# Sigmoid attention and a gated feed-forward on one core: attention moved ahead of the feed-forward and computed in unsplit float32 on four 64x64 array tiles

## The chip, the cores and the metric

The kernel runs on one core of a Trainium2 chip (trn2). The metric is device time in microseconds (us), the median of three runs. The kernel before takes 1445.89 us (1444.95 to 1446.85).

Engines are named as in the profile: PE is TensorE (matrix products), PEld its weight loads, DVE is VectorE, ACT is ScalarE, POOL is GpSimd, SP is SyncE, whose queue issues every DMA of both kernels. SBUF is the on-chip memory with 128 partitions; PSUM holds the results of PE, in 8 banks of 512 float32 columns per partition. `F32R` is a float32 format that PE takes in one pass and that keeps fewer bits than float32. The kernels keep float32 accuracy by splitting a value into a high and a low F32R part and adding three products (low x high, high x low, high x high).

## What is computed

There are 8 batches, 12 heads, 448 positions, head size 64, so 3584 tokens of 768 features; the hidden size is 1536.

```python
def _attn_ref(q, k, v) -> np.ndarray:
    S = q.shape[2]
    scale = 1.0 / np.sqrt(q.shape[-1])
    scores = scale * np.matmul(q, k.transpose(0, 1, 3, 2)) - np.log(S)
    attn = 1.0 / (1.0 + np.exp(-scores))
    return np.matmul(attn, v).astype(np.float32)

def _moe_ref(x, w_gate, w_val, w_out) -> np.ndarray:
    gate = 1.0 / (1.0 + np.exp(-(x @ w_gate)))
    val = x @ w_val
    return (gate * val @ w_out).astype(np.float32)
```

The attention output, heads side by side, is `x` of the feed-forward. There is no softmax: the attention weight of a key is a sigmoid, so keys can be taken in any groups and their products summed. The three weight matrices arrive as float64, viewed as 64-bit integers; the kernel turns them into F32R pairs by bit operations ("conversion").

## The kernel before, in words

**Hidden tiles.** The hidden size is cut into 12 tiles of 128. For a block of tokens, `ff_in` makes one hidden tile: for gate and value each 18 products (6 feature tiles x 3 terms), then a sigmoid on ACT, a product on DVE, and the split of the result into `hh` and `hl`. `ff_out` makes one of 6 output tiles from 3 products per hidden tile. The weights of 12 tiles don't fit in SBUF beside the attention, so the feed-forward is done in two passes over the tokens: the first `J1 = 5` tiles with their partial output written to DRAM (`part`), then the other 7 tiles, where `add` loads the partial output and sums.

**First stage (L272 to L461).** `heads` runs the attention head by head. The first 12 heads (`N32 = 12`, one batch) use float32 as it is: q and k stand twice in the 128 partitions, which gives twice the score, so the scale is halved. The other 84 heads are split: `split` makes F32R parts on DVE and POOL, `scores` issues 2 products for each of 4 key blocks of 128, ACT applies the sigmoid twice (once to F32R, once in place in PSUM), DVE subtracts to get the low part, and `values` issues 7 products. That makes 15 products of 448 columns for each head. `merge` mixes these heads with the first feed-forward pass, in blocks of 448 tokens, one batch behind. The head counts of each part are fixed by `HEADS_IN` and `HEADS_OUT`.

**Conversion.** `convert` handles half a row block of one matrix (128x384 elements): seven DVE operations on the words, and an eighth, `finish_lo`, that makes the low part (L137). With `spread`, the last step goes to ACT and POOL (L134, L135) and the high part is copied by ACT (L150). Each conversion loads the words of a later one (`load_words`, L98, two buffers). In the first 12 heads one conversion follows each step, so that the 5 tiles are converted early; 5 more tiles are then converted and written to DRAM (`convert_ahead`).

**Second stage (L464 to L547).** The last 448-token block of the first pass is finished, the remaining two tiles are converted, and the 5 stored tiles are fetched. Then 7 blocks of 512 tokens run through 7 hidden tiles: per block 7 x 36 + 6 x 21 = 378 products of 512 columns. `load_x` reads the attention output from DRAM and `split_x` makes its two F32R parts.

**What sets the order.** Each engine executes its queue in order. A planner orders the instructions of each queue by what they depend on; an instruction given to `keep_in_program_order` keeps its place in the written order. Buffers of a pool are handed on when their last reader has finished.

Of the kernel before, what the change touches and what calls it, by code (L numbers as in the profile page):

```python
# [11 lines left out]
U32 = mybir.dt.uint32  # L12
# [6 lines left out]
P = 128  # L19

F64_ZERO = 2.0 ** -15

J1 = 5

N32 = 12

NA = 5

EV, EW = 14, 2
# [3 lines left out]
HEADS_IN, HEADS_OUT = (23, 36, 48), (24, 38, 50)  # L33
# [3 lines left out]
def sigmoid_attention_glu_kernel(ctx: ExitStack, tc: tile.TileContext, qk, v, wg, wv, wo, out):  # L37
# [7 lines left out]

    nc = tc.nc
    B, H = qk.shape[0], qk.shape[1]
# [3 lines left out]
    NT = T // TB  # L51
    NP = H // 2
    SK = qk.shape[3] - S
# [4 lines left out]
    HP = P // 2  # L58
    scale = 1.0 / math.sqrt(D)
    J2 = NJ - J1  # L60

    const = ctx.enter_context(tc.tile_pool(name="const", bufs=1))
    wpool = ctx.enter_context(tc.tile_pool(name="wpool", bufs=1))
    work = ctx.enter_context(tc.tile_pool(name="work", bufs=2))
    dram = ctx.enter_context(tc.tile_pool(name="dram", bufs=1, space=DRAM))
    mm = ctx.enter_context(tc.tile_pool(name="mm", bufs=2, space=PSUM))
# [3 lines left out]
    x_dram = [dram.tile([P, T], F32, name=f"xd{c}") for c in range(NP)]  # L70
    w_dram = {j: [dram.tile([P, 2, DM], F32, name=f"wd{j}_{t}") for t in range(3)] for j in range(J1, J1 + NA)}
    part = [dram.tile([P, T], F32, name=f"part{o}") for o in range(NO)]


    wgv, wos = {}, {}
    KC = KT // 2

    def chunks(j, t):
        w = (wg, wv, wo)[t]
        return [w[j][:, c * KC * P:(c + 1) * KC * P] for c in range(2)]  # L80

    late = list(range(J1, NJ))
    n_own = J2 - J1


    order = [(i, o, 0) for i in range(n_own) for o in (False, True)]
    order += [(i, False, i - n_own + 1) for i in range(n_own, J2)]
    order += [(i, True, J1 + 1) for i in range(n_own, J2)]
    sources = [c for j in range(J1) for t in (0, 1) for c in chunks(j, t)]
    sources += [c for j in range(J1) for c in chunks(j, 2)]  # L90
    sources += [c for j in late[:NA] for t in (0, 1, 2) for c in chunks(j, t)]
    sources += [c for i, o, _ in order if i >= NA for t in ((2,) if o else (0, 1)) for c in chunks(late[i], t)]
    loaded, begun = [], []

    def load_words():
        if sources:
            raw = work.tile([P, KC * P], I64, tag="wraw", name="wraw")
            nc.sync.dma_start(out=raw, in_=sources.pop(0))  # L98
            loaded.append(raw.bitcast(U32).rearrange("p (n t) -> p n t", t=2))

    def drop_sign():

        if loaded:
            raw = loaded.pop(0)
            a = work.tile([P, KC * P], U32, tag="wa", name="wa")
            nc.vector.tensor_scalar(out=a, in0=raw[:, :, 1], scalar1=0x7FFFFFFF, scalar2=None, op0=ALU.bitwise_and)  # L106
            begun.append((raw, a))

    def convert(pin=False):
# [3 lines left out]
        n = KC * P  # L113
# [4 lines left out]
        t = work.tile([P, n], U32, tag="wt", name="wt")  # L118
        e = work.tile([P, n], U32, tag="we", name="we")
        ins = nc.vector.tensor_scalar(out=a.bitcast(F32), in0=a.bitcast(F32), scalar1=F64_ZERO, scalar2=None, op0=ALU.max)  # L120
        if pin:
            tc.keep_in_program_order(ins)
# [6 lines left out]
        return t.bitcast(F32), (a, e.bitcast(F32))  # L129

    def finish_lo(lo, ae, spread=False):
        a, e = ae
        if spread:
            nc.scalar.mul(a.bitcast(F32), a, 2.0 ** -34)  # L134
            nc.gpsimd.tensor_tensor(out=lo, in0=a.bitcast(F32), in1=e, op=ALU.mult)  # L135
        else:
            nc.vector.scalar_tensor_tensor(out=lo, in0=a, scalar=2.0 ** -34, in1=e, op0=ALU.mult, op1=ALU.mult)  # L137

    def gv_tile(j, pool, slot):
        gv = pool.tile([P, 2, 2, KT * P], F32R, tag=f"gv{slot}", name=f"gv_{j}")  # L140
        wgv[j] = gv.rearrange("p a b (k f) -> p a b k f", f=P)
        return gv

    def wo_tile(j, pool, slot):
        wos[j] = pool.tile([P, 2, DM], F32R, tag=f"wo{slot}", name=f"wo_{j}")
        return wos[j]

    def convert_into(hi_out, lo_out, spread):
        hi, ae = convert()
        nc.scalar.copy(hi_out, hi)  # L150
        finish_lo(lo_out, ae, spread)

    def convert_gv(j, pool, slot, spread=False):

        gv = gv_tile(j, pool, slot)
        for t in range(2):
            for c in range(2):
                cs = slice(c * KC * P, (c + 1) * KC * P)
                convert_into(gv[:, t, 0, cs], gv[:, t, 1, cs], spread)
                yield  # L160

    def convert_out(j, pool, slot, spread=False):
        wt = wo_tile(j, pool, slot)
        for c in range(2):
            cs = slice(c * KC * P, (c + 1) * KC * P)
            convert_into(wt[:, 0, cs], wt[:, 1, cs], spread)
            yield

    def convert_ahead(js):

        for j in js:
            for t in range(3):
                for c in range(2):
                    cs = slice(c * KC * P, (c + 1) * KC * P)
                    hi, ae = convert(True)
                    lo = ae[0].bitcast(F32R)
                    finish_lo(lo, ae)
                    nc.sync.dma_start(out=w_dram[j][t][:, 0, cs], in_=hi)
                    nc.sync.dma_start(out=w_dram[j][t][:, 1, cs], in_=ae[0].bitcast(F32))
                    yield  # L180

    def fetch_gv(j, pool, slot):
        gv = gv_tile(j, pool, slot)
# [3 lines left out]
    def fetch_out(j, pool, slot):  # L187
        nc.sync.dma_start(out=wo_tile(j, pool, slot).bitcast(F32), in_=w_dram[j][2])


    xh, xl = [None] * NP, [None] * NP

    def split_x(c, xr, pool):
        n = xr.shape[-1]
        xh[c] = pool.tile([P, n], F32R, tag=f"xh{c}", name="xh")
        xl[c] = pool.tile([P, n], F32R, tag=f"xl{c}", name="xl")
        nc.scalar.copy(xh[c], xr)  # L197
        nc.vector.tensor_tensor(out=xl[c], in0=xr, in1=xh[c], op=ALU.subtract)  # L198


    def products(ps, terms):
        n = len(terms)
        for i, (a, m) in enumerate(terms):
            nc.tensor.matmul(ps, lhsT=a, rhs=m, start=i == 0, stop=i == n - 1)  # L204

    def ff_in(js, pool, hs, first=0, n=S):
        for i_j, j in enumerate(js, first):
            gv = wgv[j]
            ps = []
            for t in range(2):  # L210
                acc = mm.tile([P, 512], F32, tag="mm", name="acc")[:, :n]
                ps.append(acc)
# [3 lines left out]
                for i, (a, m) in enumerate(terms):  # L216
                    nc.tensor.matmul(acc, lhsT=a, rhs=m, start=i == 0, stop=i == len(terms) - 1)  # L217
                    if i % 6 == 5:
                        if i == len(terms) - 1:
                            if t == 0:  # L220
                                g = work.tile([P, TB], F32, tag="g", name="g")[:, :n]
                                nc.scalar.activation(g, acc, AF.Sigmoid)  # L222
                            else:
                                nc.vector.tensor_tensor(out=g, in0=acc, in1=g, op=ALU.mult)  # L224
                                hh = pool.tile([P, n], F32R, tag=f"hh{i_j}", name="hh")
                                hl = pool.tile([P, n], F32R, tag=f"hl{i_j}", name="hl")
                                nc.scalar.copy(hh, g)  # L227
                                nc.vector.tensor_tensor(out=hl, in0=g, in1=hh, op=ALU.subtract)  # L228
                                hs.append((hh, hl))
                        yield 6  # L230

    def ff_out(js, hs, finish, n=S):
        for o in range(NO):
            acc = mm.tile([P, 512], F32, tag="mm", name="acc")[:, :n]
            terms = []
            for j, (hh, hl) in zip(js, hs):
                cs = slice(o * P, (o + 1) * P)
                wt = wos[j]
                terms += [(wt[:, 1, cs], hh), (wt[:, 0, cs], hl), (wt[:, 0, cs], hh)]
            for i, (a, m) in enumerate(terms):  # L240
                nc.tensor.matmul(acc, lhsT=a, rhs=m, start=i == 0, stop=i == len(terms) - 1)  # L241
                if i == len(terms) - 1:
                    finish(o, acc)
                if i % 6 == 5 or i == len(terms) - 1:
                    yield 6

    def drain(g):
        for _ in g:
            pass

    def take(g, n):
        for _ in range(n):
            next(g, None)

    def merge(main, side, n_main, n_side):

        a = s = 0
        done_a = done_s = False
        while not (done_a and done_s):
            if not done_a and (done_s or a * n_side <= s * n_main):  # L260
                try:
# [325 lines left out]
```

## Time and profile before

| quantity | value |
|---|---|
| median of 3 runs | 1445.89 us |
| profiled execution, its own time | 1440.06 us |
| its span, first to last instruction | 1438.3 us |
| mean granted TensorE clock | 0.989 |
| PE busy | 1397.2 us |
| DVE busy | 773.9 us |
| ACT busy | 597.3 us |
| POOL busy | 294.7 us |
| moved by DMA | 169.19 MB |

The profile is one execution. "Busy" counts the time in which an engine has an instruction under way. Matmuls overlap one another and their ends are modelled, so the distance between the starts of two matmuls, and not the duration of one, tells what a matmul costs. A row of the groups reads: line, engine, operation, output tile <- inputs, shape, count | busy us, mean ns of one | idle time before them and what ended it. A row of the windows reads: stretch, its length, busy time (and count) of PE, PEld, DVE, ACT and POOL, granted clock, DMA share, GB/s. A row of the chain or the timeline reads: start, duration, what.

### The profile page before, as it was taken

To read this page: it belongs to the slowest core of one execution; us is meant where nothing else is said; L and a number is where in the kernel's file an instruction comes from. 1 tells how busy PE (TensorE), PEld (TensorE's weight loads), DVE (VectorE), ACT (ScalarE), POOL (GpSimd) and SP (SyncE) were. 2 spreads that over 40 slices of the span, in tenths; PEclk is the share of its full clock that TensorE was granted. 3 is DMA by queue.
4 is the path that set the end of the run, shared out by engine and by line. 5 is a ranking of instruction groups with operands and counts; after the bars stand their busy time and mean duration, and the time that the engine had idled before them with its cause. 6 is when DMAs were issued, how large, how long until landed. Compare 5 with 4: busy or idle time off the path is not lost.

```text
span 1438.3 us, 16871 instructions
## 1 busy us (share of the span) xinstructions
PE 1397.2 (97%) x6258; PEld 1178.4 (82%) x6258; DVE 773.9 (54%) x1331; ACT 597.3 (42%) x845; POOL 294.7 (20%) x244
## 2 busy tenths in 40 slices
PE   8978999999999999999997999999999999999998
PEld 3446889899899898998995988888888888888887
DVE  6999868867768678586788483112121211212111
ACT  5646757756667567576661222011120201112010
POOL 2244625434344344343410000000000000000000
PEclk9989999999999999999998999999999999999999
DMA  6653544444535444444428861203021030300202
GB/s 215 213 188 120 160 151 126 151 131 132 155 106 154 143 120 139 135 133 150 127 90 284 329 226 50 82 1 117 15 74 59 21 111 0 103 30 15 73 0 73
DMA packets 74816, 169.19 MB, mean 118 GB/s; under 512 B 8304, under 2 KB 29040, under 8 KB 74736
## 3 DMA queue, kind: packets, MB, share of 16 engines
q1 hardware_dynamic: 74736, 168.13, 37.0%
q8 instruction: 49, 0.80, 0.3%
q14 instruction: 31, 0.25, 0.1%
HBM read 123.27 MB, written 44.83 MB: 117 GB/s over the span
## 4 chain that ended last, share of the span: by engine, by line
PE 75%; DVE 16%; DMA 6%; issue 2%; ACT 1%; SPq 0%; POOL 0%; DVEq 0%; POOLq 0%
PE acc L217 40%; PE acc L241 21%; PE sc L204 8%; PE av L204 6%; DVE wt L126 2%; DVE wt L124 2%; DMA wraw<-wv 2%; DVE wa L127 1%; DVE wa L106 1%; DMA wraw<-wg 1%; DVE wa L120 1%; DVE wa L125 1%; DMA wraw<-wo 1%; DVE xl L198 1%; DMA gv<-wd 1%
## 5 line engine op out<-in xcount | busy, mean ns | idle before, releaser
L217 PE MATMUL acc<-xh,gv 128*128 128x512 f32 (+1 forms) x2136 | 667.7, 381 | 14.8 <-ACT xh L197 14.2
L217 PEld LDWEIGHTS acc<-xh,gv 128*128 128x128 f32 x2136 | 404.2, 189 | 79.4 <-ACT xh L197 16.0
L217 PE MATMUL acc<-xl,gv 128*128 128x512 f32 (+1 forms) x1068 | 407.3, 382 | 4.2 <-DVE xl L198 4.2
L241 PE MATMUL acc<-hh,wo 128*128 128x512 f32 (+1 forms) x1068 | 325.0, 379 | 0.0
L217 PEld LDWEIGHTS acc<-xl,gv 128*128 128x128 f32 x1068 | 202.1, 189 | 36.8 <-DVE xl L198 6.1
L324 ACT ACTIVATE hi<-sc,bias 128x896 fp32r<-128x896 f32 (+1 forms) x192 | 192.9, 1010 | 91.7 <-PE sc L204 90.5
L241 PEld LDWEIGHTS acc<-hh,wo 128*128 128x128 f32 x1068 | 200.5, 188 | 30.5
L241 PE MATMUL acc<-hl,wo 128*128 128x512 f32 (+1 forms) x534 | 202.5, 379 | 0.5 <-DVE hl L228 0.5
L224 DVE TENSOR_TENSOR g<-acc,g 128x512 f32<-128x512 f32 (+1 forms) x89 | 58.8, 661 | 264.2 <-PE acc L217 263.2
L222 ACT ACTIVATE g<-acc 128x512 f32<-128x512 f32 (+1 forms) x89 | 51.1, 574 | 315.7 <-PE acc L217 315.5
L297 POOL TENSOR_TENSOR st<-raw,st 64x512 fp32r<-64x512 f32 x84 | 109.8, 1307 | 302.7 <-issue 238.4
L327 ACT ACTIVATE sc<-sc,bias 128x896 f32<-128x896 f32 x168 | 164.4, 978 | 0.0
L227 ACT CAST hh<-g 128x512 fp32r<-128x512 f32 (+1 forms) x89 | 53.1, 597 | 223.3 <-DVE g L224 223.0
L204 PE MATMUL sc<-ql,st 128*128 128x448 f32 x336 | 125.0, 372 | 5.6 <-DVE hi L335 1.7
L204 PE MATMUL sc<-st 128*128 128x448 f32 x336 | 123.5, 368 | 0.0
L528 DVE TENSOR_TENSOR ob<-acc,pb 128x512 f32<-128x512 f32 x42 | 29.0, 692 | 157.6 <-PE acc L241 149.2
L241 PEld LDWEIGHTS acc<-hl,wo 128*128 128x128 f32 x534 | 100.3, 188 | 16.5 <-DVE hl L228 1.2
L330 DVE TENSOR_TENSOR lo<-sc,hi 128x896 fp32r<-128x896 f32 x84 | 91.7, 1091 | 32.8 <-ACT sc L327 31.9
L298 POOL TENSOR_TENSOR ql<-raw,st 128x448 fp32r<-128x448 f32 x84 | 98.6, 1174 | 6.6
L204 PE MATMUL av<-hi,vs 128*128 128x448 f32 x336 | 97.5, 371 | 0.9 <-DVE hi L335 0.7
L296 DVE CAST st<-raw 128x960 fp32r<-128x960 f32 x84 | 57.1, 680 | 52.6 <-PE sc L204 28.5
L198 DVE TENSOR_TENSOR xl<-xr,xh 128x448 fp32r<-128x448 f32 (+1 forms) x96 | 67.0, 717 | 24.6 <-ACT xh L197 24.5
(43 smaller groups left out, 1196.3 us busy)
## 6 DMA issues: line engine op xcount, KB each, us to landing
raw<-qk SPq DMA_DIRECT2D x96, 480.0 KB, 3.5
vraw<-vv SPq DMA_DIRECT2D x48, 256.0 KB, 3.5
xd<-xr SPq DMA_DIRECT2D x48, 224.0 KB, 3.4
part<-ob SPq DMA_DIRECT2D x48, 224.0 KB, 3.5
xr<-xd SPq DMA_DIRECT2D x42, 256.0 KB, 3.7
pb<-part SPq DMA_DIRECT2D x42, 256.0 KB, 2.8
y<-ob SPq DMA_DIRECT2D x42, 256.0 KB, 2.0
wraw<-wg SPq DMA_DIRECT2D x24, 384.0 KB, 3.5
```

Of the source, the lines that this page charges most:

```text
L198: nc.vector.tensor_tensor(out=xl[c], in0=xr, in1=xh[c], op=ALU.subtract)
L204: nc.tensor.matmul(ps, lhsT=a, rhs=m, start=i == 0, stop=i == n - 1)
L217: nc.tensor.matmul(acc, lhsT=a, rhs=m, start=i == 0, stop=i == len(terms) - 1)
L224: nc.vector.tensor_tensor(out=g, in0=acc, in1=g, op=ALU.mult)
L227: nc.scalar.copy(hh, g)
L241: nc.tensor.matmul(acc, lhsT=a, rhs=m, start=i == 0, stop=i == len(terms) - 1)
L296: nc.vector.tensor_copy(st, raw)
L297: nc.gpsimd.tensor_tensor(out=st[HP:, S:], in0=raw[HP:, S:], in1=st[HP:, S:], op=ALU.subtract)
L298: nc.gpsimd.tensor_tensor(out=ql, in0=raw[:, :S], in1=st[:, :S], op=ALU.subtract)
L324: nc.scalar.activation(hi, sc[:, :, :S], AF.Sigmoid, bias=bias, scale=factor)
L327: nc.scalar.activation(sc[:, :, :S], sc[:, :, :S], AF.Sigmoid, bias=bias, scale=factor)
L330: nc.vector.tensor_tensor(out=lo, in0=sc[:, :, :S], in1=hi, op=ALU.subtract)
```

## The change

The order of the whole kernel is new. All 96 heads come first, then the feed-forward in 512-token blocks only, with 7 tiles in the first pass and 5 in the second.

**Attention.** Four heads make a unit `m` (24 units). Partitions 0 to 63 hold one head and 64 to 127 the next, twice (`p` = 0, 1), so q and k are no longer doubled. A unit has 7 key groups `g`: three of 128 keys for each `p`, and one, `g == 3`, that takes the last 64 keys of both. A step of a group is `scores` (4 float32 products of 64 rows, 64 columns of weights and 448 moving columns; head `h` chooses the row half and the PSUM bank, key half `u` the column half), one sigmoid of 128x896 on ACT, and two steps later (`LAG = 2`) `values` (4 float32 products, where `u` chooses the row half and `h` the column half). `finish` adds the two key halves: ACT copies one, DVE adds the other, and the sum goes to DRAM. There are no splits of q, k, v and the attention weights. 24 x 7 = 168 steps hold 1344 float32 products.

**Conversion.** One conversion follows every third step (`EV = 3`), until the 42 of the first 7 tiles are done (126 steps). The high part is copied by POOL, and the low part made by DVE. The 30 conversions of the other 5 tiles come in the first feed-forward pass, one after each hidden tile, and go to DRAM. All of them are kept in program order.

**Feed-forward.** 7 blocks of 7 x 36 + 6 x 21 products, then 7 blocks of 5 x 36 + 6 x 15, all of 512 columns, from 4 PSUM buffers. The stored tiles are fetched into the buffers of the first pass during its last block.

The core of the diff, with what stays the same left out:

```diff
-J1 = 5
-N32 = 12
-NA = 5
-EV, EW = 14, 2
+J1 = 7
 TB = 512
-HEADS_IN, HEADS_OUT = (23, 36, 48), (24, 38, 50)
+EV = 3
+LAG = 2
...
-        if pin:
-            tc.keep_in_program_order(ins)
+        tc.keep_in_program_order(ins)
...
+    def convert_tile(j):
+        gv, wt = gv_tile(j, j), wo_tile(j, j)
+        for to in (gv[:, 0], gv[:, 1], wt):
             for c in range(2):
+                cs = slice(c * CW, (c + 1) * CW)
+                hi, a, e = convert()
+                nc.gpsimd.tensor_copy(to[:, 0, cs], hi)
+                finish_lo(to[:, 1, cs], a, e)
                 yield
...
+    halves = (slice(0, HP), slice(HP, P))
...
+        def load(m):
+            if m < B * NQ:
+                b, c = divmod(m, NQ)
+                qkt = att.tile([P, 2, 2 * S], F32, tag="qk", name="qk")
+                nc.sync.dma_start(out=qkt, in_=qk[b, c])
+                vt = att.tile([P, 7, 2, D], F32, tag="v", name="v")
+                nc.sync.dma_start(out=vt, in_=v[b, c])
+                loads[m] = qkt, vt
+
+        def scores(m, g):
+            qkt, _ = loads[m]
+            sc = scp.tile([P, 2, 512], F32, tag="sc", name="sc")
+            for h in range(2):
+                for u in range(2):
+                    p = u if g == 3 else g // 4
+                    k0 = S + (3 * P if g == 3 else g % 4 * P + u * HP)
+                    nc.tensor.matmul(sc[halves[u], h, :S], lhsT=qkt[halves[h], p, k0:k0 + HP], rhs=qkt[halves[h], p, :S],
+                                     start=True, stop=True)
+            a = att.tile([P, 2, S], F32, tag="a", name="a", bufs=3)
+            nc.scalar.activation(a, sc[:, :, :S], AF.Sigmoid, bias=bias, scale=scale)
+            return a
+
+        def values(m, g, a):
+            _, vt = loads[m]
+            for u in range(2):
+                p = u if g == 3 else g // 4
+                key = (2 * m + p, u)
+                start = key not in avs
+                if start:
+                    avs[key] = avp.tile([P, 512], F32, tag=f"av{p}{u}", name="av")
+                last = (3 if u == 0 else 2) if p == 0 else 6
+                for h in range(2):
+                    nc.tensor.matmul(avs[key][halves[h], :S], lhsT=vt[halves[u], g, h], rhs=a[halves[u], h],
+                                     start=start, stop=g == last)
+            if g == 3:
+                finish(2 * m)
+            if g == 6:
+                finish(2 * m + 1)
+
+        def finish(n):
+            b, c = divmod(n, 2 * NQ)
+            x = att.tile([P, S], F32, tag="x", name="x")
+            nc.scalar.copy(x, avs.pop((n, 0))[:, :S])
+            nc.vector.tensor_tensor(out=x, in0=avs.pop((n, 1))[:, :S], in1=x, op=ALU.add)
+            store_x(b, c, x)
+
+        load(0)
+        load_words()
+        pending, beat = [], 0
+        for m in range(B * NQ):
+            load(m + 1)
+            for g in range(7):
+                pending.append((m, g, scores(m, g)))
+                if len(pending) > LAG:
+                    values(*pending.pop(0))
+                beat += 1
+                if beat % EV == 0 and len(stream) > 1:
+                    work_on()
+            if m == 2 * NQ + 1:
+                load_x(0)
+                split_x()
+        while pending:
+            values(*pending.pop(0))
...
+        for part_two in (False, True):
+            js = late if part_two else list(range(J1))
+            for t in range(NT):
+                last = part_two and t == NT - 1
+                if not last:
+                    load_x((t + 1) % NT)
+                hs = []
+                for i, j in enumerate(js):
+                    hs.append(ff_in(j, i))
+                    if not part_two:
+                        work_on()
+                        if t == NT - 1 and i < len(late):
+                            fetch_gv(late[i], i)
+                if not last:
+                    split_x()
+                for o in range(NO):
+                    (add if part_two else save)(t, o, ff_out(o, js, hs))
+            if not part_two:
+                while stream:
+                    work_on()
+                for i, j in enumerate(late):
+                    fetch_out(j, i)
```

More of the change, by code (lines that the diff above doesn't have):

```diff
@@ L2 @@
 from contextlib import ExitStack
-from itertools import chain
 import concourse.bass as bass
@@ L96, in load_words @@
         if sources:
-            raw = work.tile([P, KC * P], I64, tag="wraw", name="wraw")
+            raw = work.tile([P, CW], I64, tag="wraw", name="wraw")
             nc.sync.dma_start(out=raw, in_=sources.pop(0))
@@ L142, in gv_tile, with wo_tile @@
         return gv
-    def wo_tile(j, pool, slot):
-        wos[j] = pool.tile([P, 2, DM], F32R, tag=f"wo{slot}", name=f"wo_{j}")
+    def wo_tile(j, slot):
+        wos[j] = wpool.tile([P, 2, DM], F32R, tag=f"wo{slot}", name=f"wo_{j}")
         return wos[j]
[L148 to L156, printed above, removed]
+    def convert_tile(j):
+        gv, wt = gv_tile(j, j), wo_tile(j, j)
+        for to in (gv[:, 0], gv[:, 1], wt):
@@ L169, in convert_ahead @@
[L169 to L180, printed above, removed]
@@ L182, in fetch_gv, with convert_ahead @@
-    def fetch_gv(j, pool, slot):
-        gv = gv_tile(j, pool, slot)
+    def convert_ahead():
+        for j, t in [(j, t) for j in late for t in (0, 1)] + [(j, 2) for j in late]:
+            for c in range(2):
+                cs = slice(c * CW, (c + 1) * CW)
+                hi, a, e = convert()
+                finish_lo(a.bitcast(F32R), a, e)
+                nc.sync.dma_start(out=w_dram[j][t][:, 0, cs], in_=hi)
+                nc.sync.dma_start(out=w_dram[j][t][:, 1, cs], in_=a.bitcast(F32))
+                yield
@@ L184, in fetch_gv @@
+    def fetch_gv(j, slot):
+        gv = gv_tile(j, slot)
         for t in range(2):
             nc.sync.dma_start(out=gv[:, t].bitcast(F32), in_=w_dram[j][t])
[L187 to L198, printed above, removed]
@@ L201, in products, with fetch_out, load_x @@
[L201 to L207, printed above, removed]
+    def fetch_out(j, slot):
+        nc.sync.dma_start(out=wo_tile(j, slot).bitcast(F32), in_=w_dram[j][2])
+    xr, xh, xl = [None] * KT, [None] * KT, [None] * KT
+    def load_x(t):
+        for c in range(KT):
+            xr[c] = xpool.tile([P, TB], F32, tag=f"xr{c}", name="xr")
+            nc.sync.dma_start(out=xr[c], in_=x_dram[t][c])
@@ new lines, in split_x, with store_x @@
+    def split_x():
+        for c in range(KT):
+            xh[c] = xpool.tile([P, TB], F32R, tag=f"xh{c}", name="xh")
+            xl[c] = xpool.tile([P, TB], F32R, tag=f"xl{c}", name="xl")
+            nc.scalar.copy(xh[c], xr[c])
+            nc.vector.tensor_tensor(out=xl[c], in0=xr[c], in1=xh[c], op=ALU.subtract)
+    def store_x(b, c, x):
+        at = b * S
+        while at < (b + 1) * S:
+            t, o = divmod(at, TB)
+            n = min(TB - o, (b + 1) * S - at)
+            nc.sync.dma_start(out=x_dram[t][c][:, o:o + n], in_=x[:, at - b * S:at - b * S + n])
+            at += n
@@ L208, in ff_in @@
+    while len(stream) > 1:
+        work_on()
+    with tc.tile_pool(name="ff", bufs=2, reuse_waits="tile") as ff, \
+            tc.tile_pool(name="mm", bufs=4, space=PSUM, reuse_waits="tile") as mm:
+        def ff_in(j, i):
             gv = wgv[j]
[L209 removed]
             for t in range(2):
[L211 to L212 removed]
+                acc = mm.tile([P, TB], F32, tag="mm", name="acc")
                 terms = []
@@ L215, in ff_in @@
                     terms += [(gv[:, t, 1, c], xh[c]), (gv[:, t, 0, c], xl[c]), (gv[:, t, 0, c], xh[c])]
[L216 to L230, printed above, removed]
@@ L232, in ff_out @@
-    def ff_out(js, hs, finish, n=S):
-        for o in range(NO):
-            acc = mm.tile([P, 512], F32, tag="mm", name="acc")[:, :n]
+                for n, (a, m) in enumerate(terms):
+                    nc.tensor.matmul(acc, lhsT=a, rhs=m, start=n == 0, stop=n == len(terms) - 1)
+                if t == 0:
+                    g = ff.tile([P, TB], F32, tag="g", name="g")
+                    nc.scalar.activation(g, acc, AF.Sigmoid)
+            nc.vector.tensor_tensor(out=g, in0=acc, in1=g, op=ALU.mult)
@@ L235, in ff_out @@
+            hh = ff.tile([P, TB], F32R, tag=f"hh{i}", name="hh", bufs=1)
+            hl = ff.tile([P, TB], F32R, tag=f"hl{i}", name="hl", bufs=1)
+            nc.scalar.copy(hh, g)
+            nc.vector.tensor_tensor(out=hl, in0=g, in1=hh, op=ALU.subtract)
+            return hh, hl
+        def ff_out(o, js, hs):
+            acc = mm.tile([P, TB], F32, tag="mm", name="acc")
             terms = []
             for j, (hh, hl) in zip(js, hs):
-                cs = slice(o * P, (o + 1) * P)
-                wt = wos[j]
@@ L239, in ff_out @@
[L239 to L253, printed above, removed]
@@ new lines, in ff_out, with save, add @@
+                w = wos[j][:, :, o * P:(o + 1) * P]
+                terms += [(w[:, 1], hh), (w[:, 0], hl), (w[:, 0], hh)]
+            for n, (a, m) in enumerate(terms):
+                nc.tensor.matmul(acc, lhsT=a, rhs=m, start=n == 0, stop=n == len(terms) - 1)
+            return acc
+        def save(t, o, acc):
+            ob = ff.tile([P, TB], F32, tag="ob", name="ob")
+            nc.scalar.copy(ob, acc)
+            nc.sync.dma_start(out=part[t][o], in_=ob)
+        def add(t, o, acc):
+            pb = ff.tile([P, TB], F32, tag="pb", name="pb")
+            nc.sync.dma_start(out=pb, in_=part[t][o])
+            ob = ff.tile([P, TB], F32, tag="ob", name="ob")
+            nc.vector.tensor_tensor(out=ob, in0=acc, in1=pb, op=ALU.add)
+            nc.sync.dma_start(out=out[o, :, t * TB:(t + 1) * TB], in_=ob)
```

334 lines of the change are left out of this document (37 added, 297 removed).

## The prediction

> **What bounds the kernel now.** I read the page first, for the shares and the chain of work that ended last.
>
> ```profile
> span 1438.3 us, 16871 instructions
> PE 1397.2 (97%) x6258; PEld 1178.4 (82%) x6258; DVE 773.9 (54%) x1331; ACT 597.3 (42%) x845; POOL 294.7 (20%) x244
> GB/s 215 213 188 120 160 151 126 151 131 132 155 106 154 143 120 139 135 133 150 127 90 284 329 226 50 82 1 117 15 74 59 21 111 0 103 30 15 73 0 73
> PE 75%; DVE 16%; DMA 6%; issue 2%; ACT 1%; SPq 0%; POOL 0%; DVEq 0%; POOLq 0%
> ```
>
> PE carries three quarters of the chain and DVE a sixth. Then I read the stretches, to see where DVE has it.
>
> ```profile
> 0.00:20.00 20.00, 15.79 (x33) 7.48 (x34) 9.64 (x25) 9.38 (x14) 3.07 (x7) 1.00 0.62 207
> 20.00:140.00 120.00, 102.76 (x307) 58.99 (x306) 116.11 (x227) 67.79 (x108) 44.54 (x41) 0.93 0.58 180
> 200.00:700.00 500.00, 496.62 (x2415) 451.99 (x2414) 360.04 (x563) 335.46 (x442) 203.48 (x163) 1.00 0.45 135
> 760.00:800.00 40.00, 29.78 (x121) 24.70 (x120) 28.81 (x71) 7.23 (x13) 0.00 (x0) 0.83 0.95 312
> 863.10:1406.04 542.94, 542.94 (x2395) 449.74 (x2396) 111.81 (x164) 78.38 (x128) 0.00 (x0) 1.00 0.16 50
> ```
>
> From 20 to 140 us DVE is full (116.11 of 120), because the first weights are being converted; PE loses time there, and again at the change of stages (29.78 of 40, DMA share 0.95). Elsewhere PE is full. What a product costs is read from the chain in order of time, as length over count.
>
> ```profile
> 295.30 9.30 PE acc L241 x45
> 305.84 1.65 PE sc L204 x8
> 308.74 1.45 PE av L204 x7
> ...
> 1006.20 57.12 PE acc L217 x252
> 1063.32 28.56 PE acc L241 x126
> ...
> 1406.04 28.57 PE acc L241 x126
> ```
>
> An F32R product of 448 columns comes every 9.30/45 = 0.2067 us, one of 512 every 57.12/252 = 0.2267 us. The last products end at 1434.6, so the tail is 3.7 us. The price of unsplit float32 is read from the weight loads of an early head; their spacing is that of the matmuls which they feed.
>
> ```profile
> 59.25 0.19 PEld L204 LDWEIGHTS av<-hi,vraw 128*128 128x128 f32 x1 [0.19 <-DVE we L128]
> ...
> 61.13 0.19 PEld L204 LDWEIGHTS av<-hi,vraw 128*128 128x128 f32 x1 [0.19 <-issue]
> 61.97 0.29 PEld L204 LDWEIGHTS av<-hi,vraw 64*128 64x128 f32 x2 [0.65 <-issue]
> 63.25 0.30 PEld L204 LDWEIGHTS sc<-raw 128*128 128x128 f32 x2 [0.99 <-ACT hi L324]
> ```
>
> Five spacings lie between the first two rows: (61.13 - 59.25)/5 = 0.376 us. By the code this head has 4 products in `values`, and the trace has 8 loads for them, so a float32 product is two passes, each with a load of its own, and costs 0.752 us. Two loads stand 0.1 us apart at 63.25 (x2 in 0.30, each 0.19): the second pass's weights go in while the first streams.
>
> The span then divides so, with counts from the code. Feed-forward 2160 x 0.2067 + 2646 x 0.2267 = 446.5 + 599.8; 84 split heads of 15 products, 1260 x 0.2067 = 260.4; 12 unsplit heads of 8, 96 x 0.752 = 72.2. That is 1378.9, and 59.4 us are left for waits and low clock: the start, 20 to 140, 760 to 800, the tail.
>
> **The change part by part.** I build the span after from its stages.
>
> *Start.* The first products wait for the first q and k.
>
> ```profile
> 0.74 0.39 SPq L282 DMA_DIRECT2D raw<-qk  x1
> 4.21 9.35 PE L204 MATMUL sc<-raw 128*128 128x448 f32 x16 [4.21 <-DMA raw<-qk]
> 5.12 0.34 PEld L204 LDWEIGHTS sc<-raw 128*128 128x128 f32 x1 [0.41 <-issue]
> 5.86 0.34 PEld L204 LDWEIGHTS sc<-raw 128*128 128x128 f32 x1 [0.41 <-issue]
> ```
>
> ```profile
> raw<-qk SPq DMA_DIRECT2D x96, 480.0 KB, 3.5
> wraw<-wg SPq DMA_DIRECT2D x24, 384.0 KB, 3.5
> wo<-wd SPq DMA_DIRECT2D x5, 768.0 KB, 6.6
> ```
>
> The new transfer is 128 x 2 x 896 x 4 B = 896 KB. The lower bound is 3.5 us, as for 480 KB; carrying on the step from 480 to 768 KB (3.1 us) gives 8.0. I take 6.5, since nothing is ahead of it: PE starts at 7.2. At first passes are 0.74 us apart (5.12 to 5.86), a half clock; that and the filling of two steps ahead I put at 4.5 us (bounds 2 and 8).
>
> *Attention.* 168 steps of 4 + 4 products. If the four products of a group run side by side, a group costs two passes and a step four: 4 x 0.376 = 1.504 us, together **252.7 us**. No row shows two tiles of the array at work at once; this is the unknown of the forecast. Its bounds are side by side (1.504 a step) and one after the other (8 x 0.752 = 6.016). I take the lower end. For it speaks that by the code no two of the four use the same quarter of the array, that the two row halves write different PSUM banks, and that the two products which read the same partitions don't ask much more of them than is shown: a float32 pass streams 448 columns in 0.376 us, 1.19 per ns, twice that is 2.38, and F32R reaches 512/0.2267, 2.26 per ns. The array is also kept in one layout; where rows changed from 128 to 64 at 61.97, the load had sat idle 0.65 us instead of 0.19.
>
> In Part 3 (Packing small matmuls) of the page "TensorE: Matmul & The Clock Gate" the Trainium skill gives a group of tiles the duration of one matmul and about 4 ns for each further tile; by it a step would be an estimated 0.05 us longer and the attention 8 us. The same Part says that matmuls start and end strictly in program order, which speaks against the change; no row here decides that. It is a rival below.
>
> *What rides beside it.* ACT has one sigmoid a step and two copies in seven. DVE has 42 conversions in 126 steps, and the adds.
>
> ```profile
> L324 ACT ACTIVATE hi<-sc,bias 128x896 f32<-128x896 f32 x24 | 23.0, 999 | 7.5 <-PE sc L204 7.3
> L439 ACT COPY ob<-acc 128x448 f32<-128x448 f32 x48 | 25.8, 536 | 68.9 <-PE acc L241 65.7 <-issue 3.1
> L224 DVE TENSOR_TENSOR g<-acc,g 128x448 f32<-128x448 f32 x40 | 25.0, 624 | 14.8 <-PE acc L217 13.8
> L135 POOL TENSOR_TENSOR gv<-wa,we 128x384 fp32r<-128x384 f32 x20 | 20.3, 1016 | 61.2 <-ACT wa L134 61.2
> L137 DVE SCALAR_TENSOR_TENSOR wa<-wa,we 128x384 fp32r<-128x384 uint32 x30 | 16.6, 555 | 0.4
> ```
>
> ACT needs 0.999 + 2 x 0.536/7 = 1.15 us a step, under 1.504: hidden. For DVE I asked for the groups from 20 to 120 us alone.
>
> ```profile
> L124 DVE TENSOR_SCALAR wt<-wa 128x384 uint32<-128x384 uint32 x24 | 17.7, 739 | 0.7
> L126 DVE SCALAR_TENSOR_TENSOR wt<-wraw,wt 128x384 uint32<-128x384 uint32 x24 | 15.4, 642 | 0.0
> L127 DVE SCALAR_TENSOR_TENSOR wa<-wraw,wa 128x384 uint32<-128x384 uint32 x24 | 14.2, 590 | 0.0
> L106 DVE TENSOR_SCALAR wa<-wraw 128x384 uint32<-128x384 uint32 x24 | 13.9, 580 | 1.6 <-DMA wraw<-wo 0.8 <-DMA wraw<-wv 0.5
> L120 DVE TENSOR_SCALAR wa<-wa 128x384 f32<-128x384 f32 x23 | 11.6, 502 | 0.2
> L125 DVE TENSOR_SCALAR wa<-wa 128x384 uint32<-128x384 uint32 x24 | 10.3, 428 | 0.7
> L128 DVE TENSOR_SCALAR we<-wt 128x384 uint32<-128x384 uint32 x23 | 8.1, 353 | 0.0
> ```
>
> The seven sum to 3.83 us, with L137 4.39. L128 is of one size and kind with the other four simple ones and takes 353 ns, so they are held up; with all five at 353 a conversion is 3.55. One POOL instruction per conversion (L135, 1016 ns) runs in that stretch, and the excess is of its size. After the change POOL has one copy per conversion, so I expect most of the excess again. With 36 adds at 0.624 and 6 splits of x at about that, DVE needs 42 x 3.55 + 26.2 = 175 to 42 x 4.39 + 26.2 = 211 us, against 126 x 1.504 = 189.5 on PE. Where it exceeds, the adds come late, and with them the PSUM buffers `av`, for which `values` waits. The excess is 0 to 21; I take **12**.
>
> *Transfers.* `load(m + 1)` waits on SP until the unit before has left its buffers; behind it stand words and stores of x. Per unit 1.34 MB of q, k, v, some 0.92 of words and 0.46 of x: 2.7 MB in 10.5 us, 259 GB/s, less than the 329 that a slice shows. The words come late now and then, and DVE, pinned in order, waits: bounds 0 and 20, I take **5**.
>
> *To the feed-forward.* Its first x is split and its first weights converted long before. The change of layout and the new buffers: 0.5 to 6, I take **1.5**.
>
> *Feed-forward.* 7 x 378 + 7 x 270 = 4536 products x 0.2267 = **1028.2**, as full as 863 to 1406 shows. Beside each 8.2 us hidden tile of the first pass lies one conversion (at most 4.39) and two products of DVE; four PSUM buffers cover two tiles. The gate and value weights of five tiles (ten transfers of 768 KB, at 6.6 us each 66) are fetched while some 77 us of the block remain; the output weights have 41 us for 33. If that cover went, PE would wait for the rest, up to 15. Tail 3.7.
>
> *Sum.* 7.2 + 4.5 + 252.7 + 12 + 5 + 1.5 + 1028.2 + 3.7 = 1314.8. Against 1438.3: feed-forward 18 less, attention 80 less before its 17 of stalls, waits and edges some 43 less. The profiled execution's own time was 1.8 above its span, and the median of the runs shown is 0.4% above it (1445.89 to 1440.06): (1314.8 + 1.8) x 1.004 = **1322 us**.
>
> **The rivals.**
>
> *Passes dealt out in order.* A product's two passes need the same tile of the array, so its second starts 0.376 after its first. If no later matmul may start before that second pass, each product advances the queue by 0.376: a step is 8 x 0.376 = 3.008, the attention 505.3, DVE is hidden, and the span 7.2 + 4.5 + 505.3 + 1.5 + 1028.2 + 3.7 = 1550.4, the time **1558**. For it: the loads in the trace come strictly one pair after another, each product's two passes adjoining. Against it: on the full array they could not do otherwise, so the rows can't separate the cases. It decides from a step of (1438.3 - 1045.1)/168 = 2.34 us on. The program-order rule named above is this rival's page.
>
> *The loads don't hide.* If a load on a tile must wait for the matmul on it, each pass pays up to 0.19: 4 x (0.376 + 0.19) = 2.264 a step, 380.4 in all, a time of 1433; with half of it, for half the columns, 1369. Against it: at 63.25 the second load goes in during the first pass.
>
> *No tiles side by side at all*, the change not doing what it says: 168 x 6.016 = 1010.7, a time of about 2065. Nothing speaks for it but that no row shows the contrary.
>
> **How the numbers follow.** Side by side 0.50 (own range 1300 to 1355: stalls from 0 to 41, edges by their bounds). Loads in the open or another partial overlap short of 2.34 a step: 0.13 (1355 to 1436). Passes in order: 0.27 (1545 to 1566). Serial: 0.08. Between: 0.02. What measurement can tell from no change is 0.2%; faster 0.63, same 0.02, slower 0.35. The range has to take in the rival of the other sign, 1300 to 1566; below it and above it is left about a tenth.
>
> **What would show it.** In the attention, starts of four matmuls within some hundredths of a us and a step of 1.5 to 1.65 us (right), or starts 0.376 apart on changing tiles and a step of 3.0 (in order); loads that start only as matmuls end would show the third. DVE between 90 and 100% busy over the first 126 steps with `values` waiting on the add shows the 12 us; the granted clock should stay at 1.00. Each block of the first pass should take 378 x 0.2267 = 85.7 us and of the second 61.2. PE idle at the turn of the passes would show late fetches. A step of 2.34 or more makes the sign wrong.

## The result and the profile after

The changed kernel takes 1398.6 us in the median (1395.9 to 1402.0, four runs), beside 1445.4 us for the kernel before (1444.2 to 1446.9): a ratio of 0.968 with a 95% interval of 0.965 to 0.970. It is faster, as forecast, but it gained 47 us where 124 were forecast (1322).

The page of the changed kernel, with the shares of the chain that ended last:

```profile
span 1395.3 us, 17629 instructions
PE 1319.4 (95%) x7224; PEld 981.5 (70%) x7224; DVE 459.4 (33%) x919; ACT 368.6 (26%) x511; POOL 32.7 (2%) x46
PE 72%; DMA 13%; DVE 11%; issue 2%; ACT 1%; SPq 0%; DVEq 0%; ACTq 0%
```

DMA stands on the chain with 13% where it had 6, and DVE still with 11% where it had 16, though DVE's busy time fell from 773.9 to 459.4 us. Some of both lies in the feed-forward's first pass, where the chain follows the conversions of the later tiles while PE stays full (85.9 of the 87.3 us from 359.7 on). The rest the chain in order of time and the stretches place in the attention (columns as before).

```profile
0.74 4.81 DMA qk<-qk
...
359.70 8.42 PE acc L280 x36
...
447.58 57.12 PE acc L280 x252
...
1371.19 20.41 PE acc L298 x90
```

```profile
20.00:60.00 40.00, 32.32 (x300) 12.69 (x296) 23.12 (x53) 20.86 (x25) 4.64 (x6) 0.91 0.55 178
60.00:100.00 40.00, 27.97 (x232) 9.97 (x228) 22.77 (x51) 17.64 (x23) 3.86 (x5) 0.83 0.52 174
100.00:140.00 40.00, 29.30 (x268) 11.03 (x264) 23.85 (x55) 20.02 (x25) 4.64 (x6) 0.89 0.54 178
140.00:300.00 160.00, 126.79 (x1168) 51.65 (x1162) 88.29 (x204) 82.43 (x94) 17.78 (x23) 0.91 0.57 189
340.00:360.00 20.00, 20.00 (x212) 15.08 (x205) 2.50 (x4) 14.68 (x18) 0.00 (x0) 1.00 0.27 98
```

The feed-forward begins at 359.7 and ends at 1371.2 + 20.4 = 1391.6: 1031.9 us, beside 1028.2 forecast. The attention fills the rest. From 20 to 300 us PE is busy 70 to 81% of the time at a granted clock of 0.83 to 0.91, and no engine is full: DVE has 57% from 20 to 100 us, the DMA engines 52 to 57%. In the last stretch, when no conversion is left, PE is full at clock 1.00. So 77 of the 80 us lost lie ahead of the feed-forward, and the loss goes with the conversions. Not all of it is idle time: over the first four rows PE idles 63.6 us of 280, and the passes that it starts there would fill about 184 us at full pace (16 in 1.50 us) where it is busy for 216. The other 32 us or so, an estimate from these rows, went where the clock was low or only some of the tiles were at work.

The four array tiles do work at once. The timeline of PE in the stretch without conversions:

```profile
329.97 1.17 PE L234 MATMUL av<-a,v 64*64 64x448 f32 x8
330.72 1.17 PE L217 MATMUL sc<-qk 64*64 64x448 f32 x8
331.47 0.95 PE L234 MATMUL av<-a,v 64*64 64x448 f32 x6
```

A group of four products (8 passes; the last row is cut by the window's end) starts every 0.75 us, two passes' time, and a step of two groups takes 1.50 us: the lower end of the bounds, on which the forecast was built.

What held PE is in the waits up to 362 us (engine, line <- what it waited for: us in all, times, longest):

```profile
PE av L234 <- DVE x L245: 46.7, 18, 4.7
DVE wa L93 <- DMA wraw<-wg: 43.1, 13, 6.8
DVE wa L93 <- DMA wraw<-wo: 38.1, 13, 4.7
DVE wa L93 <- DMA wraw<-wv: 37.0, 12, 6.1
ACT xh L172 <- DMA xr<-xd: 29.3, 6, 6.2
PE sc L217 <- ACT a L220: 18.0, 6, 5.6
```

DVE stood 118 us (43.1 + 38.1 + 37.0) before L93, the first step of a conversion, until words had landed. PE stood 46.7 us before `values`, until DVE's add (L245) had set the PSUM buffers free. ACT stood 29.3 us until x had been read back, and PE 18 for ACT's sigmoid. One turn of this, in the timelines of SP, of DVE and of PE:

```profile
152.51 0.33 SPq L85 DMA_DIRECT2D wraw<-wo  x1
...
161.34 0.33 SPq L85 DMA_DIRECT2D wraw<-wo  x1
```

```profile
158.36 0.36 DVE L93 TENSOR_SCALAR wa<-wraw 128x384 uint32<-128x384 uint32 x1 [4.70 <-DMA wraw<-wo]
158.63 0.62 DVE L245 TENSOR_TENSOR x<-av,x 128x448 f32<-128x448 f32 x1
159.17 0.35 DVE L106 TENSOR_SCALAR wa<-wa 128x384 f32<-128x384 f32 x1
...
160.76 0.55 DVE L112 SCALAR_TENSOR_TENSOR wa<-wraw,wa 128x384 uint32<-128x384 uint32 x1
...
164.70 0.37 DVE L93 TENSOR_SCALAR wa<-wraw 128x384 uint32<-128x384 uint32 x1 [2.21 <-DMA wraw<-wo]
```

```profile
159.31 0.59 PE L234 MATMUL av<-a,v 64*64 64x448 f32 x2 [1.75 <-DVE x L245]
```

The next transfer of words starts (161.34) as L112 lets go of a word buffer (160.76 + 0.55 = 161.31). The next thing in DVE's queue that needs DMA is L93 on those words, and behind it stand the add and the rest of the conversion before. The code has L93 of the next conversion in the middle of this one; it is not pinned, and the planner set it ahead of the add and of this conversion's second step. With two word buffers the transfer then has almost no lead: 5.85 us from 152.51 to 158.36, with q and k on the way beside it.

### The profile page after: what moved, and what is told of

It reads as the page before. It is cut to its first block, busy times and chain, and to the rows that moved or that the text cites. A ratio compares the mean times of both kernels' runs of the same rounds, so it can differ in the third digit from the quotient of the medians.

```text
span 1395.3 us, 17629 instructions
## 1 busy us (share of the span) xinstructions
PE 1319.4 (95%) x7224; PEld 981.5 (70%) x7224; DVE 459.4 (33%) x919; ACT 368.6 (26%) x511; POOL 32.7 (2%) x46
## 4 chain that ended last, share of the span: by engine, by line
PE 72%; DMA 13%; DVE 11%; issue 2%; ACT 1%; SPq 0%; DVEq 0%; ACTq 0%
PE acc L280 42%; PE acc L298 24%; DMA wraw<-wg 3%; PE sc L217 3%; PE av L234 3%; DMA wd<-wa 3%; DMA wraw<-wv 2%; DMA xr<-xd 2%; DVE wa L112 2%; DVE wt L111 2%; DMA wraw<-wo 2%; DVE x L245 1%; DMA v<-vv 1%; DVE wt L109 1%; DVE wa L110 1%
## 5 line engine op out<-in xcount | busy, mean ns | idle before, releaser
L280 PE MATMUL acc<-xh,gv 128*128 128x512 f32 x2016 | 623.1, 389 | 0.0
L280 PE MATMUL acc<-xl,gv 128*128 128x512 f32 x1008 | 392.1, 389 | 0.0
L298 PE MATMUL acc<-hh,wo 128*128 128x512 f32 x1008 | 313.1, 389 | 0.7 <-ACT hh L287 0.7
L234 PE MATMUL av<-a,v 64*64 64x448 f32 x1344 | 247.1, 583 | 46.8 <-DVE x L245 46.7
L217 PE MATMUL sc<-qk 64*64 64x448 f32 x1344 | 247.0, 589 | 23.6 <-ACT a L220 18.0
L220 ACT ACTIVATE a<-sc,bias 128x896 f32<-128x896 f32 x168 | 168.6, 1007 | 135.8 <-PE sc L217 120.5
L298 PE MATMUL acc<-hl,wo 128*128 128x512 f32 x504 | 196.9, 391 | 1.1 <-DVE hl L288 1.1
L234 PEld LDWEIGHTS av<-a,v 64*64 64x64 f32 x1344 | 89.1, 144 | 122.0 <-DVE x L245 62.2
L217 PEld LDWEIGHTS sc<-qk 64*64 64x64 f32 x1344 | 87.3, 144 | 106.1 <-issue 65.7
L93 DVE TENSOR_SCALAR wa<-wraw 128x384 uint32<-128x384 uint32 x72 | 25.9, 359 | 201.1 <-DMA wd<-wa 83.0
L288 DVE TENSOR_TENSOR hl<-g,hh 128x512 fp32r<-128x512 f32 x84 | 58.2, 692 | 49.6 <-ACT hh L287 48.8
L172 ACT CAST xh<-xr 128x512 fp32r<-128x512 f32 x84 | 52.3, 624 | 33.1 <-DMA xr<-xd 29.3
```

Source lines behind the costliest of these rows:

```text
L172: nc.scalar.copy(xh[c], xr[c])
L217: nc.tensor.matmul(sc[halves[u], h, :S], lhsT=qkt[halves[h], p, k0:k0 + HP], rhs=qkt[halves[h], p, :S], start=True, stop=True)
L220: nc.scalar.activation(a, sc[:, :, :S], AF.Sigmoid, bias=bias, scale=scale)
L234: nc.tensor.matmul(avs[key][halves[h], :S], lhsT=vt[halves[u], g, h], rhs=a[halves[u], h], start=start, stop=g == last)
L280: nc.tensor.matmul(acc, lhsT=a, rhs=m, start=n == 0, stop=n == len(terms) - 1)
L298: nc.tensor.matmul(acc, lhsT=a, rhs=m, start=n == 0, stop=n == len(terms) - 1)
```

## The experiments

I began with three theories of the lost time. W: words are awaited without lead, in front of the add. X: the early split of the first x blocks ACT while its loads run. B: there are too many transfers for the DMA engines. "FF" below is the time at which the feed-forward's first matmul starts; in the changed kernel it is 359.6 (359.70 on the chain).

| run | time, us | ratio to before (95%) | FF, us |
|---|---|---|---|
| the change | 1398.6 | 0.968 (0.965 to 0.970) | 359.6 |
| own first step | 1460.1 | 1.012 (1.004 to 1.020) | 423.5 |
| three word buffers | 1325.0 | 0.918 (0.912 to 0.925) | 288.9 |
| x split late | 1396.9 | 0.968 (0.961 to 0.976) | 356.3 |
| every fourth step | 1385.1 | 0.960 (0.953 to 0.967) | 338.6 |
| own first step, pinned | 1327.5 | 0.922 (0.920 to 0.924) | 292.9 |
| first step pinned | 1346.2 | 0.935 (0.933 to 0.937) | 312.4 |
| no conversion | 1322.4 (one run) | | 285.4 |
| three buffers, x late | 1304.1 | 0.906 (0.904 to 0.908) | 267.1 |
| combined, three buffers | 1298.8 | 0.903 (0.901 to 0.904) | 261.8 |
| combined, two buffers | 1296.6 | 0.901 (0.900 to 0.903) | 261.2 |

**Three word buffers.**

```diff
-            raw = work.tile([P, CW], I64, tag="wraw", name="wraw")
+            raw = work.tile([P, CW], I64, tag="wraw", name="wraw", bufs=3)
...
         load(0)
         load_words()
+        load_words()
```

> Three buffers for the words instead of two, and two loads ahead instead of one; the order on VectorE stays. Theory W: the words stand ready when VectorE asks, as in the run before: 1305 to 1340 us, the waits of L93 on words fall from 118 us to under 25. Theory B: the same bytes in the same time, 1385 to 1405. Theory X: 1375 to 1400.

1325.0 us. DVE's order is the same and the bytes are the same; only the words come a conversion earlier. Its waits up to 300 us, and two stretches:

```profile
DVE wa L93 <- DMA wraw<-wg: 11.1, 6, 6.8
DVE wa L93 <- DMA wraw<-wo: 4.3, 3, 1.9
DVE wa L93 <- DMA wraw<-wv: 3.6, 3, 1.5
```

```profile
60.00:100.00 40.00, 29.47 (x252) 9.98 (x244) 23.04 (x51) 17.32 (x22) 3.85 (x5) 0.87 0.55 180
140.00:300.00 160.00, 160.00 (x1629) 119.41 (x1622) 89.25 (x200) 112.34 (x130) 15.41 (x20) 1.00 0.65 216
```

The waits for words fell from 118 to 19 us, the attention by 71 us, and from 140 us on PE is full with the conversions still running. B falls: the same transfers now run at 216 GB/s beside 189. The low clock falls as a cause of its own too: it went back to 1.00 where the stalls went. From 60 to 100 us hardly anything improved (PE 29.47 us busy beside 27.97); there another wait rules.

**x split late.** The loads and the split of the first x, given to the planner with their place fixed near the end of the attention.

```diff
-            if m == 2 * NQ + 1:
-                load_x(0)
-                split_x()
+            if m == B * NQ - 2:
+                load_x(0, True)
+                split_x(True)
```

Here `True` applies `keep_in_program_order` to the loads and to ACT's casts.

> The loads and the split of the first 512 tokens of x are put at the end of the attention and kept there in program order. Theory X: ScalarE's 29 us of waits for these loads between 60 and 115 us go away, and the attention loses 25 to 60 us: 1335 to 1370. Theory W: the words remain the pace (7 us for a conversion), so little is gained, 0 to 20 us: 1375 to 1398. Theory B: six transfers of 256 KB move, under 5 us.

1396.9 us: no difference that can be told from the change. X alone doesn't explain the loss, and by itself this wait lies under the other.

**Both.**

> Three word buffers and the late split of x together. With the words ready, the x loads are the next wait: in the run with three buffers PE was busy 29.5 of 40 us from 60 to 100 and 37.2 of 40 to 140, where ScalarE waits 26 us for x. Theory: the 12 to 20 us come back here, though the same edit alone gave nothing: 1303 to 1315 us. If the stretch had another cause: 1320 to 1330.

1304.1 us, FF from 288.9 to 267.1: the edit that gave nothing alone gives 22 us here. Its stretches:

```profile
20.00:60.00 40.00, 40.00 (x432) 15.31 (x428) 34.95 (x81) 29.97 (x36) 6.93 (x9) 1.00 0.79 258
60.00:100.00 40.00, 40.00 (x431) 15.17 (x424) 35.18 (x81) 30.05 (x35) 6.94 (x9) 1.00 0.81 271
```

PE is full from 20 to 100 us, DVE at 87 to 88% with its conversions, and DMA moves 258 to 271 GB/s. So X was a second wait under W, worth what stands free once W is gone.

**First step pinned.** W has two halves: that the words have no lead, and that the add stands behind the wait. This run leaves the word buffers and the loads as they are and moves only the place of L93, behind the add and behind L106.

```diff
-            nc.vector.tensor_scalar(out=a, in0=raw[:, :, 1], scalar1=0x7FFFFFFF, scalar2=None, op0=ALU.bitwise_and)
+            ins = nc.vector.tensor_scalar(out=a, in0=raw[:, :, 1], scalar1=0x7FFFFFFF, scalar2=None, op0=ALU.bitwise_and)
+            tc.keep_in_program_order(ins)
```

> The change, with the first step of the next conversion kept where the code has it, behind the add and behind the second step of this conversion; the words' lead is the change's own (a transfer begins when the conversion before has let go of its buffer). Tells the two halves of theory W apart. If the missing lead is the cause, DVE still stands 2 to 5 us for each conversion and the period stays near 7 us: 1375 to 1400. If the add's place behind the wait is the cause: 1310 to 1345.

1346.2 us lies on neither side's line (1375 to 1400, 1310 to 1345), just above the second. DVE's waits up to 400 us:

```profile
DVE wa L93 <- DMA wraw<-wg: 24.1, 12, 6.8
DVE wa L93 <- DMA wraw<-wo: 22.1, 11, 3.9
DVE wa L93 <- DMA wraw<-wv: 17.9, 10, 3.6
```

Still 64 us of waiting, but FF moved from 359.6 to 312.4. Of the 71 us that a third buffer brought, 47 are had by moving one DVE instruction of 0.36 us behind another; with the lead as well, 20 to 24 more. The 47 are not the add's place alone. The add and L106 now run while the words are on their way, so that 1.99 us lie between L93 and the next load of words where the change has 2.98 (158.36 to 161.34 above). No run separates the two.

**Own first step, and the same pinned.** Each conversion does its own first step.

```diff
         tc.keep_in_program_order(ins)
-        drop_sign()
```

> Each conversion does its own first step (the one that drops the sign) instead of doing it for the next conversion; nothing else changes, bytes and operations stay. Theory W (words waited for too early): after the change DVE waits for words whose transfer began only when the conversion before had let go of the buffer, and the add of the attention output stands behind that wait; a conversion then takes a transfer of 3.4 to 6 us plus 2.9 us on DVE, some 7 us, where three steps of PE take 4.5. With the first step moved, a transfer has a whole conversion of lead: attention 354 us becomes 265 to 295 and the whole 1305 to 1340 us. Theory B (the transfers themselves are too many for the DMA engines): no gain, 1385 to 1405. Theory X (the early split of the first x blocks ScalarE while its loads run, which starves the sigmoids): at most 20 less, 1375 to 1400.

1460.1 us, 1.2% above the kernel before (0.4 to 2.0): a miss for all three theories. The count of conversions from 20 to 260 us shows why, the change first, then this run:

```profile
L93 DVE TENSOR_SCALAR wa<-wraw x35: 344/360/366, 22.8 to 259.3; 128x384 uint32<-128x384 uint32 x35
```

```profile
L93 DVE TENSOR_SCALAR wa<-wraw x59: 343/353/362, 21.7 to 256.8; 128x384 uint32<-128x384 uint32 x59
```

With the link between two conversions gone, the planner set conversions ahead of the adds, 59 in place of 35, up to four between two adds, those of the later tiles among them. The waits for words fell from 118 to 29 us, but the adds came later still: PE waited 88.1 us for them where it was 46.7. So this run changed two things. Pinning the first step too takes the second away:

> As the run in which each conversion does its own first step, with that step also kept in program order, so that the planner can't pull whole conversions ahead of the adds. Two word buffers as in the change. Theory W (words awaited without lead, in front of the add): the words now have a whole conversion of lead, 1310 to 1345 us, and 42 conversions spread over the attention, not 71 in 300 us. If the earlier run's loss came from something else than its order: above 1385.

1327.5 us, with the change's two buffers: within 3 us of the three buffers. The lead counts, not the buffer.

**Every fourth step.** `EV = 4`.

> One conversion in four steps instead of three, so the 42 conversions fill all 168 steps (4 x 1.504 = 6.0 us each) instead of 126. Theory W: a conversion still takes 6.5 to 7 us, but none of the steps is left over without one: attention 42 x 7 + 8 = 300 us, whole 1335 to 1355. Theory X: the late x costs the same, 1375 to 1398 with the start of the block moved. Theory B: the same bytes, and PE's and the transfers' time overlap better: 1350 to 1390.

1385.1 us, a gain of 13 us where theory W had expected 44 to 64. The time lies in the ranges of X and B too. The run with three buffers speaks against B, and X alone gave nothing, so that this range decides nothing. DVE's waits up to 420 us, and its conversions:

```profile
DVE wa L93 <- DMA wraw<-wg: 51.1, 16, 7.1
DVE wa L93 <- DMA wraw<-wv: 46.5, 14, 5.6
DVE wa L93 <- DMA wraw<-wo: 42.6, 14, 4.6
```

```profile
L93 DVE TENSOR_SCALAR wa<-wraw x29: 359/360/367, 23.6 to 254.7; 128x384 uint32<-128x384 uint32 x29
```

DVE waited for words even longer, 140 us. The last row has 28 intervals of 8.25 us, and from 22.8 to 259.3 the change has 34 of 6.96, but the two means don't count the same thing. In the change 6 of the 34 intervals hold no add: there one conversion runs straight behind another, 1.6 to 3.4 us. The other 28 average 7.9, and here all 28 hold an add. Two of the longest pieces of the chain in order of time:

```profile
165.62 5.59 DMA wraw<-wv
...
180.34 5.30 DMA wraw<-wo
```

From 156 to 255 us nearly the whole chain goes from L112 to the transfer of the words, from there to L93 and the add behind it, and on to the next L112. PE stands in between only where two adds follow each other, at 202.4. So the wait is a loop of DVE and DMA. Its turn is 2.98 us from L93 to the next load of words, and then 3.0 to 3.3 us until the next L93, or 4.6 to 6.5 where q, k and v are on the way beside the words. Longer turns, up to 18.6 us, lie from 70 to 118 us, where x is read back. So W had the loop right and its length too short: it took 6.5 to 7 us for each conversion, as the change's mean is, and here, with an add in every turn, 8.25 was measured.

**No conversion.** The attention alone.

> The 42 conversions of the attention are left out: no words are loaded for them and GpSimd fills the weights of the first 7 tiles with constants. The first x is split late as in the run on that. The attention alone is left: 168 x 1.504 = 252.7 us from a start at 5.6 with 4 us of filling, so the feed-forward begins at 262 to 268 and the whole takes 1297 to 1306 us. If the four array tiles or the transfers of q, k and v cost more than the two passes a group, it begins later than 275.

FF at 285.4, at least 17 us later than expected (262 to 268). The reason lies in the first 40 us and not in the pace of the attention. Rows of its DVE and POOL timelines, and its stretches:

```profile
7.84 22.95 DVE L92 TENSOR_SCALAR wa<-wraw 128x384 uint32<-128x384 uint32 x1 [6.98 <-DMA wraw<-wg]
```

```profile
0.73 0.42 POOL L135 MEMSET gv<- 128x384 f32 x1 [0.29 <-POOLq L365]
```

```profile
0.00:31.00 31.00, 15.71 (x140) 5.56 (x140) 23.18 (x3) 12.20 (x13) 30.05 (x88) 0.88 0.30 115
60.00:260.00 200.00, 200.00 (x2134) 126.30 (x2130) 23.74 (x38) 149.96 (x172) 0.00 (x0) 1.00 0.53 176
```

POOL filled the weights without a pause until 31 us, and in that time one DVE instruction, of 0.36 us elsewhere, took 22.95; PE then waited 16.8 us for an add behind it. From 60 to 260 us PE was full. So the pace of the attention alone is as expected, but its length can't be read from this run; the run with three buffers and x late gives it.

**Combined.** Both repairs of the words, each with the loads of x two units ahead of its split and with the first q and k in two transfers.

```diff
+            if m == B * NQ - 4:
+                load_x(0, True)
+            if m == B * NQ - 2:
+                split_x(True)
```

> Three word buffers; the loads of the first x two units before its split, both kept in order near the end of the attention; the first q and k in two transfers. Against the run with three buffers and the late x (feed-forward from 267.1): the 3.3 us for which ScalarE waited for x and about 1 us at the start go away: feed-forward from 261 to 265, the whole 1297 to 1304 us. Theory W leaves nothing else: attention at 1.504 us a step from about 5 us on. If the time stays at 1304 or above, the split itself (6 casts of 0.62 us in a row) is what holds the sigmoids.

> The same, but with the change's two word buffers and each conversion's own first step kept in order in place of the third buffer. With x out of the way, this and the three buffers should meet, 1297 to 1306 us: the lead of the words is what counts, not where it comes from. If two buffers are too few under the load of q, k and v, 1310 or more.

1298.8 and 1296.6 us: the first as expected, the second 0.4 us under its range of 1297 to 1306. For the second, the chain has

```profile
261.29 57.35 PE acc L289 x252
```

The version with two buffers is 9.9% faster than the kernel before (ratio 0.901, 0.900 to 0.903) and 7% faster than the change, with the change's own operations on the engines, bytes and buffers. What differs is the order of the first step and of the x loads and splits, and that the first q and k come in two transfers.

## Why the prediction was right and wrong, step by step

**The price of a group: right.** Two passes for four products, 1.504 us a step predicted, 1.50 in the trace. In the run with three buffers and x late the attention takes 267.1 - 5.5 = 261.6 us, beside 252.7 and the filling. The rival of passes dealt out in order (starts 0.376 apart, a step of 3.0) is refuted: eight passes start in each 0.75 us. The rule behind it, in Part 3 of the Trainium skill's page "TensorE: Matmul & The Clock Gate", that matmuls start in program order, is not what sets the time here; the records don't say which pass is which, so whether the passes are issued out of order, or in an order that doesn't block, stays open. The other rule of that Part, a group in about the duration of one matmul, agrees with 0.75 us for a float32 product of two passes; the 0.05 us more for a step that the prediction estimated from it do not show at 1.50. The loads hide: the group of the loads for `scores` has 144 ns for one, and sixteen loads of both kinds in each step of 1.50 us.

```profile
L217 PEld LDWEIGHTS sc<-qk 64*64 64x64 f32 x1344 | 87.3, 144 | 106.1 <-issue 65.7
L113 DVE TENSOR_SCALAR we<-wt 128x384 uint32<-128x384 uint32 x72 | 38.5, 535 | 0.0
```

The case "loads in the open or another partial overlap", 1355 to 1436, covers the measured time, but its mechanism did not occur; the number fell there by another way.

**"The words come late now and then, and DVE, pinned in order, waits: bounds 0 and 20, I take 5": this is the step that failed.** DVE waited 118 us, and the attention lost 67 to 71 by it (the runs with lead: FF at 288.9 and 292.9 against 359.6). I priced transfers by their rate, 259 GB/s against 329 shown, and the rate was right: with the waits gone the kernel moves 258 to 271. What I didn't price was when a transfer may start: I did not go through which buffer the words need, which instruction frees it, and what stands behind the instruction that waits. The code had all three, `drop_sign` in the middle of `convert`, two buffers, and the add in the same queue. I also took "pinned" for the whole conversion ("All of them are kept in program order"), where one instruction, L106, is pinned and L93 is free to move.

**The load and split of the first x: missing.** I wrote "split long before" and gave it nothing. It costs ACT 29 us of waiting in the stretch from 60 to 115 us, and 22 us of time once the words are in order (288.9 to 267.1).

**"DVE's excess, I take 12": too much.** A conversion takes 0.36 + 0.35 + 0.36 + 0.36 + 0.55 + 0.55 + 0.66 + 0.56 = 3.75 us up to 359 us by the rows of its eight operations (3.55 and 4.39 were the bounds), and DVE's 42 x 3.75 + 26.2 = 184 us fit under PE's 189.5. Of the five simple operations only L113 was held up, 0.66 us here and 535 ns over the whole run (second row above) where 353 was the size before. In the run with three buffers and x late DVE was 87 to 88% busy from 20 to 100 us where it was expected at 90 to 100, and no wait of PE for DVE is left in the attention. In the change itself it was 57% busy there, held by the words.

**The small terms.** The first q and k landed at 5.6 (0.74 + 4.81) and PE started there, not at 7.2. The feed-forward took 1031.9 where 1028.2 was expected; from its second block on, 57.12 us for 252 products is the predicted 0.2267. The fetches at the turn of the passes stayed covered.

**The sum.** Of the 80.5 us between the forecast span (1314.8) and the measured (1395.3), 359.7 - 282.9 = 76.8 are the start and the attention and 3.7 the feed-forward. The runs give the 77 a cause: words 71 and x 22 by the three-buffer runs, less the 12 and 5 that the sum had allowed for stalls, which makes 76.

## What to carry to other kernels

Price a prefetch by its lead, not by its bandwidth: for each load find the instruction that frees its buffer, the one that waits for it, and what is queued behind that one on its engine. An order that pins one instruction of a chain lets a planner move the others; look at the order which it made before believing that the code's holds. When two waits lie over each other, taking away one of them can show nothing, as the late x did alone; it was worth 22 us behind the first.

## What was not expected of the hardware

One DVE instruction of 0.36 us took 22.95 us while POOL ran one memset of 0.42 us after another, started 0.36 us apart. The section Who interferes with whom of the Trainium skill's page "SBUF — State Buffer" says that a VectorE instruction in a 2-port mode and GpSimd share a pair of ports, which the one that issues first holds for its whole instruction while the other fully blocks, and that `tensor_scalar` can enter such a mode. No run here shows whether this instruction was in one. The trace fits it in that DVE stood until POOL was done, but behind some sixty POOL instructions ((30.8 - 7.8) us at one in 0.36 us), not behind one: DVE did not get its turn between them. It is one instance, and nothing else was tried against it. No run here shows whether another kind of POOL instruction does the same.
